# 608 slots an expert, logits by token, and half-width value products in the left units

## The chip, the cores and the metric

The kernel runs on one core of a Trainium2 chip. Its time is the device time of one execution in microseconds (us), and the median of several executions is what two kernels are compared by. A core has a matrix engine (PE, with its weight loads shown apart as PEld), a vector engine (DVE), an activation engine (ACT), a general engine (POOL, which also issues the indirect DMAs) and SP, which issues the plain DMAs. Each engine works through its own list of instructions in a fixed order; semaphores make one wait for another.

## The reference

Attention that keeps the 32 largest scores of a row, a feed-forward layer, and a mixture of experts in which each token goes to its two best experts of eight:

```python
# attention: q, k, v are (4, 8, 576, 64)
scores = scale * np.matmul(q, k.transpose(0, 1, 3, 2))
kth = np.partition(scores, -32, axis=-1)[..., -32:-31]
scores = np.where(scores >= kth, scores, -1e9)
attn = softmax(scores)
x = (attn @ v).transpose(0, 2, 1, 3).reshape(2304, 512)
# feed forward: w_in (512, 2048), w_out (2048, 512)
h = np.maximum(x @ w_in, 0.0)
x = h * h @ w_out
# mixture of experts: w1 (8, 512, 1024), w2 (8, 1024, 512)
noisy = x @ w_gate + np.log1p(np.exp(x @ w_noise)) * noise
top2 = the two largest of noisy, top2_w = softmax over them
for e in range(8):
    for k in range(2):
        mask = top2[:, k] == e
        h = np.maximum(x[mask] @ w1[e], 0.0)
        out[mask] += top2_w[mask, k, None] * (h @ w2[e])
```

## The kernel before, in words

**Attention** goes through 80 units. A full unit (`pair_full`, 64 of them) takes 128 queries of two heads. Since 576 is four and a half times 128, 64 queries of each batch and head are left over; a left unit (`pair_left`, 16 of them) takes these 64 queries of two heads at once, head A in rows 0 to 63 and head B in rows 64 to 127. `scores` (L363) makes the scores, DVE searches the 32 largest (L376 to L383), POOL and ACT make the softmax (L404, L405), `transpose4` (L417) and `rest` (L440, L441) turn the result, and `times_v` (L454) multiplies by the values: five chunks of keys times two heads, each a plain fp32 product that PE carries out as two instructions, with 64 value columns of one head as the loaded weights and 128 query columns moving through. In a left unit both heads move all 128 query columns, though `finish` (L430) reads only columns 0 to 63 of head A and 64 to 127 of head B.

**Feed forward** runs as filler between the attention steps (`ffn`, in six chunks of 384 tokens; L274 to L276 and L288 to L290) and is completed once attention has ended. Numbers that need more precision than one fp32r product gives are split into a high and a low part, so each product stands as three matmuls.

**The router** (`route`) follows each chunk. For each of its three tiles of 128 tokens it turns the tokens (L177, L179), multiplies with the 16 router columns as loaded weights and 128 tokens moving (L183), copies the 16 x 128 logits out (L184), and after the third tile turns all logits back by three small transposes (L188) and a copy (L191). The PSUM buffer `pf` that these steps and the feed-forward products use during attention is a single one. Then come small operations, and each token's row is written to two slots of `xs` by an indirect DMA (L251).

**The experts** have 640 static slots each, in five tiles of 128 that form two parts of 384 and 256 (`CAP`, `PARTS`). `fetch` reads a tile of slots, turns it (four transposes, L525) and splits it (L529, L530). `expert` runs eight steps over the 1024 hidden columns. In each step it loads and splits the weights (L567 to L572), makes 12 matmuls for the first part and 12 for the second (L578 to L580, the loaded weights being a 128 x 128 block of w1 and the tokens moving), splits the hidden values (L584, L585), and makes 15 matmuls with 512 moving columns, three for each tile (`second`, L559 to L561). At the end of an expert DVE adds each tile to the rows of the output gathered before (L599, three buffers `y`), and POOL scatters it (L600). Unused slots carry a row number beyond the end, which the indirect DMA skips. The first parts of experts 0 and 1 are worked on early, before the last chunk is routed; their second parts follow.

**Overflow**: if an expert gets more tokens than it has slots, a branch after the experts (`blank`, `beyond`) works on the rest in loops; otherwise it is jumped over.

The instructions are put in order by a list scheduler that plays the program through with modelled durations; an order number that the program gives (and the offsets `FILL_LATER` and `SOON`) decides among those that are ready.

Of the kernel before, what the change touches and what calls it, by code (L numbers as in the profile page):

```python
# [8 lines left out]
F32 = mybir.dt.float32  # L9
# [8 lines left out]
P = 128  # L18
# [34 lines left out]
def attention_ffn_moe(ctx: ExitStack, tc: tile.TileContext, q, k, v, w_ffn, w_route, noise, w_exp, out,  # L53
# [18 lines left out]
    CAP = 640  # L72
    CAPT = CAP // P
# [38 lines left out]
    nz = cpool.tile([P, NTT, E], F32, name="nz")  # L112

# [56 lines left out]
    def route(t0, xrs):  # L170

        nt = len(xrs)
        lts = fpool.tile([2 * E, CH], F32, name="lts", bufs=1)
        for i, xr in enumerate(xrs):
# [274 lines left out]
    def times_v(b, hA, pts, t5):  # L449
        av = ps_a.tile([P, 512], F32, name="pa")  # L450
        for c in range(NFULL + 1):
            for i in range(2):
                rhs = pts[i][:, c * P:(c + 1) * P] if c < NFULL else t5[:, 0, :]
                nc.tensor.matmul(av[i * D:(i + 1) * D, 0:P], V[b][c][:, hA + i, :], rhs,  # L454
                                 start=(c == 0), stop=(c == NFULL))
        return av, t5[:, 1, :]

    def pair_full(b, j, qt):
# [17 lines left out]
        yield times_v(b, hA, pts, t5)  # L476

    def pair_left(b, j, qt):
# [21 lines left out]
        yield times_v(b, hA, [pt, pt], t5)  # L500
# [14 lines left out]
    def fetch(e, parts):  # L515

        xe = [mpool.tile([P, 2, NC, n], F32R, name=f"xe{o}") for o, n in parts]
        t0, t1 = parts[0][0] // P, sum(parts[-1]) // P
        info = mpool.tile([P, CAPT, 4], F32, name="info")
        for t in range(t0, t1):  # L520
            xr = mpool.tile([P, ROW], F32, name="mr", bufs=3)
            nc.sync.dma_start(xr, xs[e * NT + t * P:e * NT + (t + 1) * P, :])
            pt = ps_m.tile([P, DM], F32, name="ph")
            for c in range(NC):
                nc.tensor.transpose(pt[:, c * P:(c + 1) * P], xr[:, c * P:(c + 1) * P], ident)  # L525
            i, off = place(parts, t)
            hi, lo = xe[i][:, 0, :, off:off + P], xe[i][:, 1, :, off:off + P]
            pv = pt.rearrange("p (c s) -> p c s", c=NC)
            nc.scalar.activation(hi, pv, AF.Copy)  # L529
            nc.vector.tensor_tensor(lo, pv, hi.bitcast(F32), op=ALU.subtract)  # L530
            gate(info[:, t, :], xr, e)
# [5 lines left out]
    def expert(e, parts, ahead):  # L537

        xe, info = found.pop(0)
        tiles_ = range(parts[0][0] // P, sum(parts[-1]) // P)  # L540
# [14 lines left out]
        def second(f, wo, hs):  # L555
            for t in tiles_:
                i, off = place(parts, t)
                sl = slice(off, off + P)
                nc.tensor.matmul(acc[t], hs[i][:, 0, sl], wo[:, 0, :], start=(f == 0), stop=False)  # L559
# [428 lines left out]
```

## Time and profile before

| what | us |
| --- | --- |
| median of three executions | 1397.62 |
| lowest and highest of them | 1397.25 to 1398.67 |
| the profiled execution | 1400.53 |
| its span, first to last instruction | 1398.8 |
| PE busy | 1272.1 (91%) |
| PEld busy | 1092.8 (78%) |
| DVE busy | 933.5 (67%) |
| ACT busy | 846.2 (60%) |
| POOL busy | 763.2 (55%) |

The profile is of one execution. Busy time of PE is modelled from pipelined matmuls: the duration of one matmul runs from its start to its last result, and the next has started long before, so what a matmul costs is read from the distance between two starts, not from its duration. The span falls into stages: attention with feed forward and conversion of weights up to about 800 us, the rest of feed forward and the early experts up to about 980 us, and the experts to the end.

### The profile page before, as it was taken

The numbers are of one execution on the slowest core, as the hardware profiler recorded it, in microseconds if no ns is written. First come the engines' busy times: TensorE is split into PE (matmuls) and PEld (weight loads), VectorE is DVE, ScalarE is ACT, GpSimd is POOL, SyncE is SP. The second block draws the span as 40 slices with busy tenths as digits, with TensorE's granted clock in tenths as the row PEclk, the third lists the DMA queues.
The fourth block names the chain that finished last, engine by engine and source line by source line (L and its number), as shares of the span: only waits on it lengthen the run. The fifth ranks groups of instructions, "written<-read, shape, count | busy, mean of one in ns | idle before, by whom it ended". The sixth has DMA issues, their size and how long they took to land.

```text
span 1398.8 us, 26295 instructions
## 1 busy us (share of the span) xinstructions
PE 1272.1 (91%) x7937; PEld 1092.8 (78%) x7937; DVE 933.5 (67%) x5089; ACT 846.2 (60%) x1757; POOL 763.2 (55%) x1238
## 2 busy tenths in 40 slices
PE   2766577999999999999999999899999999999996
PEld 1544465888888888878888888788888999989995
DVE  7999889799977999999889101145554444444342
ACT  5787898778877787988878434353443333233321
POOL 5868999655786577768647523605233405134131
PEclk9995688999999999999999999999999999999998
DMA  9985676653576355446524676837664334343241
GB/s 333 364 323 199 219 271 227 198 176 106 170 245 234 101 168 186 152 136 206 174 77 160 233 254 209 267 106 234 200 210 146 128 112 165 125 148 129 91 145 38
DMA packets 85240, 257.49 MB, mean 184 GB/s; under 512 B 10716, under 2 KB 10844, under 8 KB 85088
## 3 DMA queue, kind: packets, MB, share of 16 engines
q1 hardware_dynamic: 75808, 227.32, 48.8%
q0 software_dynamic: 9280, 28.40, 5.6%
q8 instruction: 65, 1.06, 0.3%
q14 instruction: 87, 0.71, 0.2%
HBM read 205.71 MB, written 52.06 MB: 184 GB/s over the span
## 4 chain that ended last, share of the span: by engine, by line
PE 59%; DVE 12%; DMA 4%; ACT 3%; POOL 3%; issue 2%; another core or an unknown queue 0%; SPq 0%; POOLq 0%; DVEq 0%; ACTq 0%
PE ph L579 5%; PE ph L578 5%; PE ph L580 5%; PE acc L559 5%; PE acc L561 5%; PE acc L560 5%; PE acc L276 4%; DVE w L377 3%; PE acc L274 3%; PE acc L275 3%; PE pa L454 3%; PE ps L363 3%; DVE m L376 3%; PE pa L417 2%; PE pf L288 2%; PE pf L290 2%
## 5 line engine op out<-in xcount | busy, mean ns | idle before, releaser
L404 POOL TENSOR_TENSOR sb<-sb,w 128x576 f32<-128x576 f32 x144 | 204.4, 1426 | 37.6 <-ACT w L403 36.6
L377 DVE MATCH_REPLACE8 w<-m,sb 128x96 f32<-128x96 f32 x864 | 202.5, 244 | 0.7 <-issue 0.6
L584 ACT ACTIVATE ht<-ph 128x384 fp32r<-128x384 f32 (+1 forms) x128 | 55.9, 437 | 217.3 <-PE ph L580 202.7
L585 DVE SCALAR_TENSOR_TENSOR ht<-ph,ht 128x384 fp32r<-128x384 f32 (+1 forms) x128 | 62.7, 490 | 183.7 <-ACT ht L584 171.0
L376 DVE MAX8 m<-sb 128x8 f32<-128x96 f32 x864 | 168.6, 246 | 21.7 <-ACT sb L365 15.3
L363 PE MATMUL ps<-K,qt 128*128 128x288 f32 (+2 forms) x640 | 139.9, 349 | 41.6 <-ACT sb L365 15.8
L600 POOL DMA_INDIRECT out<-y,info x40 | 45.1, 1128 | 241.3 <-DVE y L599 234.7
L578 PE MATMUL ph<-xe,wi 128*128 128x384 f32 (+1 forms) x512 | 159.9, 312 | 2.0 <-DVE xe L530 2.0
L579 PE MATMUL ph<-xe,wi 128*128 128x384 f32 (+1 forms) x512 | 160.1, 313 | 0.8 <-DVE xe L530 0.8
L580 PE MATMUL ph<-xe,wi 128*128 128x384 f32 (+1 forms) x512 | 159.4, 311 | 0.0
L363 PEld LDWEIGHTS ps<-K,qt 128*128 128x128 f32 x640 | 107.8, 215 | 58.9 <-ACT sb L365 24.3
L298 POOL TENSOR_TENSOR gt<-r,gt 128x384 fp32r<-128x384 f32 x96 | 97.2, 1014 | 84.4 <-ACT gt L297 68.6
L559 PE MATMUL acc<-wo,ht 128*128 128x512 f32 x320 | 126.7, 398 | 1.2 <-DVE y L599 0.7
L405 ACT ACTIVATE sb<-sb,keep 128x576 f32<-128x576 f32 x144 | 111.7, 776 | 23.3 <-POOL sb L404 22.8
L560 PE MATMUL acc<-wo,ht 128*128 128x512 f32 x320 | 125.4, 394 | 0.0
L403 ACT ACTIVATE w<-sb,keep 128x576 f32<-128x576 f32 x144 | 110.2, 774 | 21.7 <-POOL keep L399 19.3
L417 PE MATMUL pa<-ident,sb 128*128 128x128 f32 x576 | 101.5, 304 | 23.0 <-ACT sb L405 17.0
L288 PE MATMUL pf<-xT,wi 128*128 128x384 f32 x320 | 114.2, 357 | 4.1 <-DMA wi<-wsc 2.3
L274 PE MATMUL acc<-wo,gt 128*128 128x512 f32 x288 | 112.1, 402 | 4.8 <-DMA wo<-wsc 2.9
L289 PE MATMUL pf<-xT,wi 128*128 128x384 f32 x320 | 110.8, 346 | 2.8 <-POOL xT L432 2.7
L290 PE MATMUL pf<-xT,wi 128*128 128x384 f32 x320 | 111.0, 347 | 0.0
L275 PE MATMUL acc<-wo,gt 128*128 128x512 f32 x288 | 110.1, 396 | 0.0
(185 smaller groups left out, 3437.4 us busy)
## 6 DMA issues: line engine op xcount, KB each, us to landing
wi<-wsc SPq DMA_DIRECT2D x96, 512.0 KB, 4.9
wo<-wsc SPq DMA_DIRECT2D x96, 512.0 KB, 4.1
raww<-in_exp SPq DMA_DIRECT2D x80, 512.0 KB, 3.6
raw<-in_ffn SPq DMA_DIRECT2D x32, 512.0 KB, 4.7
wsc<-csp SPq DMA_DIRECT2D x32, 512.0 KB, 5.4
xs<-xr SPq DMA_DIRECT2D x40, 258.0 KB, 6.8
mr<-xs SPq DMA_DIRECT2D x40, 258.0 KB, 3.7
qn<-in_q SPq DMA_DIRECT2D x40, 256.0 KB, 2.8
```

The source lines that it names most:

```text
L274: nc.tensor.matmul(acc[tt], gt[:, 0, sl], wo[:, 0, :], start=(f == 0), stop=False)
L275: nc.tensor.matmul(acc[tt], gt[:, 0, sl], wo[:, 1, :], start=False, stop=False)
L288: nc.tensor.matmul(ph[:, 0:n], wi[:, 0, sl], xT[:, 0, c, 0:n], start=(c == 0), stop=False)
L363: nc.tensor.matmul(ps[:, n, 0:w], st, kt[:, at:at + w], start=(i == 0), stop=(i == len(pairs) - 1))
L376: nc.vector.max(top, sb[:, sl])
L377: nc.vector.match_replace(out=w[:, sl], in_to_replace=top, in_values=sb[:, sl], imm_value=NEG)
L404: nc.gpsimd.tensor_tensor(sb, sb, w, op=ALU.subtract)
L559: nc.tensor.matmul(acc[t], hs[i][:, 0, sl], wo[:, 0, :], start=(f == 0), stop=False)
L560: nc.tensor.matmul(acc[t], hs[i][:, 0, sl], wo[:, 1, :], start=False, stop=False)
L578: nc.tensor.matmul(ph[:, 0:n], wi[:, 0, sl], xe[i][:, 0, c, :], start=(c == 0), stop=False)
L579: nc.tensor.matmul(ph[:, 0:n], wi[:, 0, sl], xe[i][:, 1, c, :], start=False, stop=False)
L580: nc.tensor.matmul(ph[:, 0:n], wi[:, 1, sl], xe[i][:, 0, c, :], start=False, stop=(c == NC - 1))
```

## The change

Three things are changed.

1. `CAP` goes from 640 to 608. The parts are now 384 and 224, the fifth tile has 96 rows. Its transposes, matmuls, splits and the final addition are cut to 96 rows; the unused 32 rows of its `info` get a row number beyond the end, and the last 32 rows of its `y` are set to zero by a POOL memset before the addition.
2. The router's product has the turned tokens as loaded weights (128 x 128) and the 16 router columns moving, so the logits come out with a token in each row. The copy goes straight into `lgs`; the three transposes back (L188) and the copy after them (L191) are gone.
3. In a left unit, `times_v` moves only the 64 query columns of each head.

The overflow branch is adapted to a first slot that is not a multiple of 128.

```diff
-    CAP = 640
-    CAPT = CAP // P
+    CAP = 608
+    CAPT = -(-CAP // P)
     PARTS = [(0, 384), (384, CAP - 384)]
...
     def route(t0, xrs):
-        lts = fpool.tile([2 * E, CH], F32, name="lts", bufs=1)
+        lgs = fpool.tile([P, CT, 2 * E], F32, name="lgs", bufs=2)
...
-                nc.tensor.matmul(lt[0:2 * E, 0:P], wg[:, c, :], xt[:, c, :], start=(c == 0), stop=(c == NC - 1))
-            nc.scalar.copy(lts[:, i * P:(i + 1) * P], lt[0:2 * E, 0:P])
+                nc.tensor.matmul(lt[:, 0:2 * E], xt[:, c, :], wg[:, c, :], start=(c == 0), stop=(c == NC - 1))
+            nc.scalar.copy(lgs[:, i, :], lt[:, 0:2 * E])
             yield 1
-        lp = ps_f.tile([P, DM], F32, name="pf")
-        for i in range(nt):
-            nc.tensor.transpose(lp[:, 2 * E * i:2 * E * (i + 1)], lts[:, i * P:(i + 1) * P], ident[0:2 * E, 0:2 * E])
-        lgs = fpool.tile([P, CT, 2 * E], F32, name="lgs", bufs=1)
         lg = lgs[:, 0:nt, :]
-        nc.scalar.copy(lg, lp[:, 0:2 * E * nt].rearrange("p (t e) -> p t e", e=2 * E))
...
-    def times_v(b, hA, pts, t5):
+    def times_v(b, hA, pts, t5, whole):
         av = ps_a.tile([P, 512], F32, name="pa")
         for c in range(NFULL + 1):
             for i in range(2):
-                rhs = pts[i][:, c * P:(c + 1) * P] if c < NFULL else t5[:, 0, :]
-                nc.tensor.matmul(av[i * D:(i + 1) * D, 0:P], V[b][c][:, hA + i, :], rhs,
+                o, n = (0, P) if whole else (i * LEFT, LEFT)
+                rhs = pts[i][:, c * P + o:c * P + o + n] if c < NFULL else t5[:, 0, o:o + n]
+                nc.tensor.matmul(av[i * D:(i + 1) * D, o:o + n], V[b][c][:, hA + i, :], rhs,
                                  start=(c == 0), stop=(c == NFULL))
...
     def fetch(e, parts):
+            n = min(P, CAP - t * P)
-            nc.sync.dma_start(xr, xs[e * NT + t * P:e * NT + (t + 1) * P, :])
+            nc.sync.dma_start(xr[0:n], xs[e * NT + t * P:e * NT + t * P + n, :])
...
-                nc.tensor.transpose(pt[:, c * P:(c + 1) * P], xr[:, c * P:(c + 1) * P], ident)
+                nc.tensor.transpose(pt[:, c * P:c * P + n], xr[0:n, c * P:(c + 1) * P], ident[0:n, 0:n])
...
+            if n < P:
+                nc.gpsimd.tensor_copy(info[n:P, t, 3:4].bitcast(I32), far[n:P])
...
         def second(f, wo, hs):
-                sl = slice(off, off + P)
+                sl = slice(off, off + rows[t])
+                to = acc[t][0:rows[t]]
...
             y = mpool.tile([P, DM], F32, name="y", bufs=3)
-            nc.vector.scalar_tensor_tensor(y, acc[t], info[:, t, 2:3], cur[t], op0=ALU.mult, op1=ALU.add)
+            n = rows[t]
+            if n < P:
+                nc.gpsimd.memset(y[n:P], 0.0)
+            nc.vector.scalar_tensor_tensor(y[0:n], acc[t][0:n], info[0:n, t, 2:3], cur[t][0:n],
+                                           op0=ALU.mult, op1=ALU.add)
```

## Rows read from the trace of the kernel before

**Rows 1.** By stretch: length, busy us (count) of PE, PEld, DVE, ACT, POOL, clock, DMA

```profile
300.00:480.00 180.00, 176.25 (x1275) 148.96 (x1275) 152.63 (x1031) 143.12 (x312) 123.91 (x191) 1.00 0.52 175
480.00:640.00 160.00, 154.46 (x1123) 132.56 (x1120) 155.67 (x1101) 135.03 (x293) 112.92 (x185) 0.99 0.46 154
640.00:800.00 160.00, 159.39 (x1140) 137.15 (x1138) 123.46 (x845) 121.91 (x268) 102.98 (x165) 1.00 0.49 165
1100.00:1384.00 284.00, 284.00 (x1613) 256.81 (x1612) 118.82 (x199) 88.64 (x176) 81.58 (x168) 1.00 0.38 123
```

**Rows 2.** Chain that ended last, shares by line, 480 to 640 and 640 to 800 us

```profile
by line: DVE w L377 23.4%; DVE m L376 17.6%; DVE m L378 11.5%; DVE cand L383 10.1%; DVE m L381 9.2%; issue 3.8%; ACT sb L365 2.1%; ACT pt L419 1.8%; POOL sb L404 1.8%; ACT sb L405 1.6%; DVE x L426 1.5%; ACT w L403 1.5%; ACT r L296 0.9%; DVE
by line: PE pa L454 14.2%; PE pa L417 10.3%; PE ps L363 10.3%; PE acc L274 9.8%; PE pf L288 9.8%; PE pf L290 9.6%; PE acc L276 9.6%; PE pf L289 9.6%; PE acc L275 9.6%; PE pf L183 1.8%; PE pa L440 1.3%; PE pa L441 1.3%; PE pf L177 1.0%; DVE 
```

**Rows 3.** Instruction groups by form: operation, shapes, count, busy us, mean ns

```profile
L578 PE MATMUL ph<-xe,wi 128*128 128x256 f32 x256 | 73.2, 286 | 2.0 <-DVE xe L530 2.0
L363 PE MATMUL ps<-K,qt 128*128 128x64 f32 x64 | 13.0, 203 | 0.0
```

**Rows 4.** Timeline of PE within an expert: start us, duration us, instruction

```profile
1157.73 0.28 PE L578 MATMUL ph<-xe,wi 128*128 128x256 f32 x1
...
1159.15 0.40 PE L559 MATMUL acc<-wo,ht 128*128 128x512 f32 x1
...
1161.00 0.34 PE L578 MATMUL ph<-xe,wi 128*128 128x384 f32 x1
...
1163.12 0.86 PE L561 MATMUL acc<-wo,ht 128*128 128x512 f32 x3
```

**Rows 5.** Chain of 707 to 736 us, a left unit: start us, us, what

```profile
712.23 1.29 PE ps L363 x8
...
713.77 1.02 PE pa L454 x16
...
715.91 0.37 PE pa L454 x4
...
716.87 0.98 PE pf L183 x8
```

**Rows 6.** Timeline of PE, the router's count products

```profile
948.47 0.17 PE L222 MATMUL pf<-mb,onesb 128*128 128x8 bf16 x1
948.50 0.17 PE L223 MATMUL pf<-mb,tri 128*128 128x8 bf16 x1
```

**Rows 7.** Timeline of PE around one set of transposes back

```profile
937.93 0.34 PE L578 MATMUL ph<-xe,wi 128*128 128x384 f32 x1
938.20 0.35 PE L188 MATMUL pf<-ident,lts 16*128 16x16 f32 x3
...
938.77 0.34 PE L580 MATMUL ph<-xe,wi 128*128 128x384 f32 x1
```

**Rows 8.** Copies of a left unit's scores: count, min/median/max ns, first and last start

```profile
L367 ACT ACTIVATE sb<-ps x16: 570/597/625, 136.6 to 725.2; 128x512 f32<-128x512 f32 x16
```

**Rows 9.** Timeline of the end: DVE's additions and POOL's scatters

```profile
1390.99 1.46 DVE L599 SCALAR_TENSOR_TENSOR y<-acc,info,cur 128x512 f32<-128x512 f32 x2 [3.64 <-DMA out<-y,info]
1392.02 0.98 POOL L600 DMA_INDIRECT out<-y,info  x1 [0.95 <-DVE y L599]
1393.30 0.98 POOL L600 DMA_INDIRECT out<-y,info  x1 [0.30 <-issue]
```

**Rows 10.** Timeline between two experts: additions of the fourth and fifth tile, next product

```profile
1160.03 0.74 DVE L599 SCALAR_TENSOR_TENSOR y<-acc,info,cur 128x512 f32<-128x512 f32 x1
...
1163.82 0.40 PE L559 MATMUL acc<-wo,ht 128*128 128x512 f32 x1
```

**Rows 11.** Indirect DMA by window: packets, MB; expert 1's second part, expert 7 whole

```profile
q0 software_dynamic: 160, 0.43, 15.2%
...
q0 software_dynamic: 400, 1.21, 22.9%
```

**Rows 12.** Instruction groups: POOL clearing a whole 128x512 tile

```profile
L545 POOL MEMSET cur<- 128x512 f32 x6 | 2.9, 528 | 0.1
```

More of the change, by code (lines that the diff above doesn't have):

```diff
@@ L112, in attention_ffn_moe @@
     nz = cpool.tile([P, NTT, E], F32, name="nz")
+    far = cpool.tile([P, 1], F32, name="far")
+    nc.gpsimd.memset(far, float(2 * NT))
     wctx = ctx.enter_context(ExitStack())
@@ L475, in pair_full @@
         yield
-        yield times_v(b, hA, pts, t5)
+        yield times_v(b, hA, pts, t5, True)
     def pair_left(b, j, qt):
@@ L499, in pair_left @@
         yield
-        yield times_v(b, hA, [pt, pt], t5)
+        yield times_v(b, hA, [pt, pt], t5, False)
     def place(parts, t):
@@ L517, in fetch @@
         xe = [mpool.tile([P, 2, NC, n], F32R, name=f"xe{o}") for o, n in parts]
-        t0, t1 = parts[0][0] // P, sum(parts[-1]) // P
+        t0, t1 = parts[0][0] // P, -(-sum(parts[-1]) // P)
         info = mpool.tile([P, CAPT, 4], F32, name="info")
@@ L521, in fetch @@
             xr = mpool.tile([P, ROW], F32, name="mr", bufs=3)
-            nc.sync.dma_start(xr, xs[e * NT + t * P:e * NT + (t + 1) * P, :])
+            n = min(P, CAP - t * P)
+            nc.sync.dma_start(xr[0:n], xs[e * NT + t * P:e * NT + t * P + n, :])
             pt = ps_m.tile([P, DM], F32, name="ph")
             for c in range(NC):
-                nc.tensor.transpose(pt[:, c * P:(c + 1) * P], xr[:, c * P:(c + 1) * P], ident)
+                nc.tensor.transpose(pt[:, c * P:c * P + n], xr[0:n, c * P:(c + 1) * P], ident[0:n, 0:n])
             i, off = place(parts, t)
-            hi, lo = xe[i][:, 0, :, off:off + P], xe[i][:, 1, :, off:off + P]
-            pv = pt.rearrange("p (c s) -> p c s", c=NC)
+            hi, lo = xe[i][:, 0, :, off:off + n], xe[i][:, 1, :, off:off + n]
+            pv = pt.rearrange("p (c s) -> p c s", c=NC)[:, :, 0:n]
             nc.scalar.activation(hi, pv, AF.Copy)
             nc.vector.tensor_tensor(lo, pv, hi.bitcast(F32), op=ALU.subtract)
-            gate(info[:, t, :], xr, e)
+            gate(info[0:n, t, :], xr[0:n], e)
+            if n < P:
+                nc.gpsimd.tensor_copy(info[n:P, t, 3:4].bitcast(I32), far[n:P])
             yield None
@@ L539, in expert @@
         xe, info = found.pop(0)
-        tiles_ = range(parts[0][0] // P, sum(parts[-1]) // P)
+        tiles_ = range(parts[0][0] // P, -(-sum(parts[-1]) // P))
+        rows = {t: min(P, CAP - t * P) for t in tiles_}
         cur = {}
@@ L557, in second @@
                 i, off = place(parts, t)
-                sl = slice(off, off + P)
-                nc.tensor.matmul(acc[t], hs[i][:, 0, sl], wo[:, 0, :], start=(f == 0), stop=False)
-                nc.tensor.matmul(acc[t], hs[i][:, 0, sl], wo[:, 1, :], start=False, stop=False)
-                nc.tensor.matmul(acc[t], hs[i][:, 1, sl], wo[:, 0, :], start=False, stop=(f == NFE - 1))
+                sl = slice(off, off + rows[t])
+                to = acc[t][0:rows[t]]
+                nc.tensor.matmul(to, hs[i][:, 0, sl], wo[:, 0, :], start=(f == 0), stop=False)
+                nc.tensor.matmul(to, hs[i][:, 0, sl], wo[:, 1, :], start=False, stop=False)
+                nc.tensor.matmul(to, hs[i][:, 1, sl], wo[:, 0, :], start=False, stop=(f == NFE - 1))
                 yield True, 0.5
@@ L818, in attention_ffn_moe @@
     nc.vector.tensor_copy(first, row_i)
-    far = cpool.tile([P, 1], F32, name="far")
-    nc.gpsimd.memset(far, float(2 * NT))
     any_extra = nc.values_load(extra[0:1, E:E + 1], min_val=0, max_val=NT + P)
@@ L836, in blank @@
         nc.vector.tensor_tensor(taken, row, base[:, e:e + 1], op=ALU.is_lt)
+        outside = opool.tile([P, 1], F32, name="outside")
+        nc.vector.tensor_scalar(outside, row, float((e + 1) * NT), None, op0=ALU.is_ge)
+        nc.vector.tensor_tensor(taken, taken, outside, op=ALU.add)
         nc.vector.tensor_scalar(taken, taken, float(E * NT), None, op0=ALU.mult)
@@ L896, in attention_ffn_moe @@
                 nc.vector.tensor_scalar(row, first, float(e * NT), None, op0=ALU.add)
-                with tc.For_i(0, (NT - CAP) // P, 1):
+                with tc.For_i(0, -(-(NT - CAP) // P), 1):
                     blank(e, row, none)
```

## The prediction

> **What bounds the kernel now.** I read the busy time by stretch first, then the chain of what ended last in the same stretches, then the starts of single matmuls. From 1100 to 1384 us, six experts and part of a seventh, PE is busy without a gap at the full granted clock while DVE, ACT and POOL are busy less than half of the time [rows 1]. What PE saves there comes off the time one for one. From 640 to 800 us PE is busy 159.4 of 160 us, DVE 123.5, and the head of the chain is PE work alone [rows 1, 2]. From 480 to 640 us it is the other way round: DVE is busy 155.7 of 160 us and the chain is the search for the largest scores [rows 1, 2]; PE time saved in that stretch buys nothing. From 300 to 480 us PE is busy 176.3 of 180 us, with DVE at 152.6 behind it [rows 1]: mostly PE, with little room before DVE is next. The change touches PE's instructions in both kinds of stretch, and almost nothing of DVE's.
>
> **How a matmul is priced.** I take the distance between starts. Twelve matmuls of 256 columns take 1157.73 to 1159.15, 0.118 us each; eight of 512 take until 1161.00, 0.231 each; twelve of 384 take until 1163.12, 0.177 each [rows 4]. So a column costs some 0.45 ns with a small constant, and 224 columns would cost 0.118 - 32 x 0.00045 = 0.104 us. But each matmul also needs its own 128 x 128 block of weights loaded, and that has a floor. The scores of a left unit show it: four matmuls of 512 columns alternate with four of 64 [rows 3], and the eight take 1.29 us [rows 5]. Four of 512 are 0.93; the other four take 0.36, although 64 columns cost only about 0.03. The first 64-column matmul finds its weights loaded during the 512 before it (0.03); the other three wait about 0.11 each, the load behind a matmul too short to cover it. **A 128-column load cannot be repeated faster than about 0.111 us**, and 224 columns fall below this.
>
> **608 slots, first products.** The three lines have 256 matmuls of 256 columns each [rows 3], 768 in all, of which each goes from 0.118 to the floor of 0.111: 768 x 0.007 = 5.4 us. Ends: 768 x 0.014 = 10.8 us if the columns decide, nothing if the load already sets 0.118. I take the load's floor, since its row has the same kind of weights and is the nearest. The 64-column form also shows that fewer than 256 columns don't fall into a slower mode: four passes over 64 columns would not fit into 0.03 us.
>
> The Trainium skill ("TensorE: Matmul & The Clock Gate", Back-to-back issue gap, and LDWEIGHTS) gives a warm gap of N/2.4 + 2.5 ns and a load of columns/1.2 ns, so by it 256 columns cost 109 ns and the load 107: narrowing would gain 2 ns each, 1.5 us in all. The trace disagrees on the first figure, with 118 ns at 256 columns; this is the rival named B below.
>
> **608 slots, the rest.** The 15 products of the second kind still move 512 columns; 96 instead of 128 loaded columns lie under 0.231 us of moving: nothing. Four transposes of the fifth tile in each of eight experts move a quarter less: plain fp32 work takes 0.108 us for 128 columns (eight in 0.98, less the change of kind [rows 5]), so at most 32 x 0.027 = 0.9 us, and I take 0.6 (loads may hold it; end 0). ACT's and DVE's narrower splits lie beside a saturated PE, with DVE busy 42% there [rows 1]: nothing. POOL gets a copy and a memset for each expert. A memset of a whole tile takes 0.53 us [rows 12]; the one here covers 32 partitions but as many columns. It must wait until the second tile's scatter has read the same `y` buffer (three buffers, fifth tile), and behind it on POOL stand the fifth tile's scatter and the next expert's gathers. DVE's fifth addition now waits for it, and the next expert's matmul into that PSUM tile waits for the addition. Between experts this has room: the fifth addition starts at 1160.03 and lasts 0.74, the matmul starts at 1163.82 [rows 10], so 3 us lie free, and a memset queued behind the fourth scatter needs about 1. At the very end nothing covers it: the fourth scatter runs 1392.02 to 1393.00, and the fifth starts at 1393.30 since its addition was long done [rows 9]. With the memset (0.53) and the addition (0.75) in between it starts at about 1394.6, 1.3 us later; if the scheduler puts the memset ahead of the fourth scatter it costs nothing. I take 0.7 us, added. Slots suffice: expert 1's second part moves 0.43 MB in 2048-byte rows, about 208 beyond its 384, 592 in all; expert 7 moves 1.21 MB, 591 [rows 11], and the same windows of the other six show no more. All are below 608, so the overflow branch stays jumped over.
>
> **Left units.** From sixteen instructions in 1.02 us and four in 0.37 [rows 5], a pair of instructions (head A and head B, in different column halves) costs (1.02 - 0.37)/6 = 0.108 us, and the change of kind before them 0.15. Half the columns would halve the moving to 0.054; the load of 64 columns, half of 0.111, is about 0.055 (estimate), and the two loads of a pair go to different halves. Instructions can follow at this rate: two matmuls with loads of their own start 0.03 apart [rows 6], a pair 0.06. So 0.058 a pair, and the ten pairs of a unit save 0.5 us. The 16 left units run from 136.6 to 725.2 us [rows 8] in four groups of four, by batch: about 136 to 204, 309 to 354, 409 to 473 and 676 to 726 us. The first group runs before PE is the bound, the other three in the PE stretches. 12 x 0.5 = 6.0, and because DVE is close behind in the 300 to 480 stretch I count 5.0 us. Ends: nothing (DVE or loads hold it), 16 x 0.52 = 8.3.
>
> **Router.** One set of transposes back in expert surroundings: 937.93 to 938.77 for two products of 0.177 and the three transposes, so they cost 0.84 - 0.35 = 0.49 us with the changes of kind around them [rows 7]; where other plain fp32 work stands beside them, about 0.3. Six chunks give some 2.4, of which I count 1.8, as one or two lie in the DVE stretch; ends 0 and 2.9. The copy after them and a step on the single `pf` buffer go as well, beside other work. The turned product itself: eight instructions take 0.98 [rows 5], 0.108 each plus the change of kind. Now a 128-column load stands where 128 columns moved, 0.111 each: 18 x 8 x 0.003 = 0.4 us more, taken as 0.3; ends 0 and, if the loads don't overlap with the short matmuls at all, another 0.03 each, 4 us.
>
> **Sum.** 5.4 + 0.6 + 5.0 + 1.8 - 0.7 - 0.3 = 11.8 us off. Against the profiled execution: 1400.5 to 1388.7. That execution was 0.2% above the median, so against the median 1397.6 - 11.8 = **1386 us**.
>
> **Rivals.**
> A. *DVE takes over in attention.* The left units and the router save PE time, but DVE is 85% busy at 300 to 480 and 97% after [rows 1], so only the third group of left units and the last two chunks count: 2.0 + 0.8 instead of 6.8, 4.0 less, 1390. For it: the DVE stretch follows directly. Against: the chain at 640 to 800 is PE's. Chance 0.23.
> B. *The load already sets 0.118 at 256 columns,* so the narrower products bring nothing: 1391. Against it: 256, 384 and 512 columns lie on one line [rows 4], which a load floor would break, and the alternating scores give 0.111. Chance 0.10; the skill's figures above lead here.
> C. *Columns decide,* the load is no floor: 5.4 more, 1380. Only the scores' rows speak against it. Chance 0.10.
> D. *Another order of the work.* The scheduler plays the whole program through, so changed durations of the router and left units from 130 us on may change the order of everything behind them, attention's balance of PE and DVE included. PE's gaps from 300 to 640 us are 9 us [rows 1]; an order that doubles them takes most of the gain: 1395. Chance 0.07; an order that closes them goes the other way, about 1378, chance 0.05.
> E. *Slower: POOL's memset holds PE.* If the wait for the scatter's landing and POOL's queue delay the fifth addition beyond the 3 us of room [rows 10], PE stands at each of the seven expert boundaries. To lose more than 11.8 + 2.8 us it takes 2 us at each, a delay of 5 us: only if POOL has the memset behind the next expert's gathers. Then 1401. Chance 0.04.
> F. *Slower: fewer than 256 columns run in a slow mode,* at the rate of the plain fp32 rows (0.108 for 128 columns in each of two instructions [rows 5]): 224 columns would take 0.38 us, 768 x 0.26 = 200 us more, 1590. The 64-column form speaks against it. Chance 0.02.
>
> **How the numbers follow.** The forecast has 0.39; its own range is 1382 to 1389.5. What a measurement of this kernel can tell from no change is 0.2%, 2.8 us: 1394.8 to 1400.4. Forecast, A, B, C, the better half of D and half of its worse half are faster: 0.39 + 0.23 + 0.10 + 0.10 + 0.05 + 0.02 = 0.89; I keep a little for delays that no row shows: 0.85 faster, 0.08 the same, 0.07 slower. The range reaches over C below and most of D above: 1378 to 1395.
>
> **What would show it.** Right: starts of 224-column matmuls 0.111 apart, pairs of 64-column value products 0.058 apart, L188 gone, an expert 0.7 us shorter, attention ending 5 to 7 us earlier, the last scatter about a microsecond later after PE's end. Wrong: starts 0.104 or 0.118 apart; attention ending where it did with more idle PE; PE idle before a product into the fifth tile at the expert boundaries; new gaps in feed forward at 800 to 980 us; any work in the overflow branch.

## The result, and the profile after

The changed kernel takes 1410.7 us (1408.3 to 1416.5), the kernel before 1397.6 beside it: a ratio of 1.0080 (95% interval 1.0056 to 1.0104). It is slower by some 11 to 13 us, where 11.8 us less were forecast. The profiled execution took 1408.5 us, of which the span is 1406.8, against 1400.5 and 1398.8 before.

What the prediction said of single instructions came out as written. In the timeline of PE inside an expert (start us, duration us, instruction), twelve matmuls of 224 columns take from 1203.83 to 1205.16, 0.111 us each, where [rows 4] had 0.118:

```profile
1203.19 0.34 PE L583 MATMUL ph<-xe,wi 128*128 128x384 f32 x1
...
1203.83 0.27 PE L581 MATMUL ph<-xe,wi 128*128 128x224 f32 x1
...
1205.16 0.41 PE L562 MATMUL acc<-wo,ht 128*128 128x512 f32 x1
```

In the chain of what ended last (start us, us, what) from 460 to 469 us, a left unit's scores take 1.29 us as before, its values 0.61 and 0.27 instead of 1.02 and 0.37 [rows 5], and the router's product 0.80 instead of 0.98:

```profile
460.83 1.29 PE ps L360 x8
462.12 0.61 PE pa L452 x16
...
464.35 0.27 PE pa L452 x4
...
467.22 0.80 PE pf L185 x8
```

A pair of value products costs (0.61 - 0.27)/6 = 0.057 us (forecast 0.058), a unit saves 0.51 us (0.5), and a full expert, measured between the last additions of neighbouring experts, takes 57.4 to 58.1 us (four of them) where it took 57.9 to 58.8. These pieces of work became shorter by what was forecast, and the router's part by more. The loss lies elsewhere. The table by stretch (length; busy us of PE, PEld, DVE, ACT, POOL; granted clock; DMA) shows that PE stands idle more:

```profile
300.00:480.00 180.00, 172.71 (x1237) 146.98 (x1235) 147.98 (x1005) 137.03 (x301) 119.58 (x183) 0.98 0.50 171
480.00:640.00 160.00, 152.58 (x1104) 133.19 (x1102) 153.59 (x1068) 133.14 (x289) 113.36 (x188) 0.98 0.47 158
640.00:800.00 160.00, 157.36 (x1141) 135.91 (x1140) 133.28 (x898) 122.16 (x268) 103.41 (x166) 1.00 0.48 166
800.00:980.00 180.00, 169.81 (x923) 151.82 (x923) 41.52 (x117) 76.14 (x153) 71.17 (x155) 0.99 0.63 211
980.00:1100.00 120.00, 109.86 (x636) 95.25 (x636) 59.61 (x106) 47.48 (x96) 35.23 (x93) 0.94 0.52 172
1100.00:1384.00 284.00, 284.00 (x1631) 253.01 (x1631) 120.38 (x203) 89.87 (x179) 86.38 (x179) 1.00 0.39 126
```

The kernel before, in the two stretches that [rows 1] doesn't have:

```profile
800.00:980.00 180.00, 173.41 (x916) 150.53 (x914) 45.95 (x124) 76.84 (x151) 67.90 (x148) 0.99 0.65 216
980.00:1100.00 120.00, 113.74 (x668) 101.72 (x667) 60.64 (x105) 47.27 (x95) 35.48 (x91) 0.97 0.53 174
```

Length less PE's busy time is PE idle: from 300 to 1100 us it is 37.7 us after and 22.8 before, 14.9 more, spread over every stretch but the last. That sum alone doesn't tell what was lost: with the same work in the order of before it is 35.0 us in a faster kernel (below), so much of it is saved work that became idle time. The granted clock, a mean of its two levels of 1.2 and 2.4 GHz as a share of the upper one, fell as well: 0.98, 0.98 and 0.94 instead of 1.00, 0.99 and 0.97 in the first, second and fifth stretch. Lengths times the missing clock are 15.8 us after and 7.0 before, so up to 8.8 us of full-speed work more were lost in that way; PE had idled more in those stretches. The end costs 1.3 us more: from the start of the last two additions to the end of the span 9.1 us, before 7.8 [rows 9]. The clearing of `y` stands there as feared, between the last two scatters:

```profile
1398.75 0.97 POOL L607 DMA_INDIRECT out<-y,info  x1 [0.83 <-DVE y L605]
1399.71 0.55 POOL L604 MEMSET y<- 32x512 f32 x1
1400.54 0.97 POOL L607 DMA_INDIRECT out<-y,info  x1 [0.28 <-POOL y L604]
```

By milestones of the two profiled executions, in us after less us before: last scores +18.7 (782.9 against 764.2), last second-layer product of the feed forward +7.6, last scatter into `xs` +5.9, first addition of expert 0's second part +9.7, of expert 1's second part +11.1, last pair of additions of the last expert +6.7, the span +8.0. So attention ends much later with part of the feed forward done earlier, the experts' first boundaries lose 5 us more, and the full experts win 4 back.

### The profile page after: what moved, and what is told of

It is laid out like the page before. It is cut to its first block, busy times and chain, and to the rows that moved or that the text cites. A ratio compares the mean times of both kernels' runs of the same rounds, so it can differ in the third digit from the quotient of the medians.

```text
span 1406.8 us, 26264 instructions
## 1 busy us (share of the span) xinstructions
PE 1263.8 (90%) x7919; PEld 1086.3 (77%) x7919; DVE 934.5 (66%) x5089; ACT 840.0 (60%) x1751; POOL 767.5 (55%) x1254
## 4 chain that ended last, share of the span: by engine, by line
PE 60%; DVE 13%; DMA 13%; POOL 5%; ACT 4%; issue 3%; SPq 1%; another core or an unknown queue 0%; POOLq 0%; DVEq 0%; ACTq 0%
PE acc L562 5%; PE acc L564 5%; PE acc L563 5%; PE ph L583 5%; PE ph L582 5%; PE ph L581 5%; DVE w L374 4%; PE pa L452 4%; PE acc L271 4%; PE acc L272 3%; PE acc L273 3%; DMA xs<-xr 3%; PE ps L360 3%; PE pf L285 3%; DVE m L373 3%
## 5 line engine op out<-in xcount | busy, mean ns | idle before, releaser
L374 DVE MATCH_REPLACE8 w<-m,sb 128x96 f32<-128x96 f32 x864 | 205.5, 255 | 0.1
L373 DVE MAX8 m<-sb 128x8 f32<-128x96 f32 x864 | 171.7, 257 | 28.8 <-ACT sb L362 25.9
L562 PE MATMUL acc<-wo,ht 128*128 128x512 f32 (+1 forms) x320 | 127.5, 402 | 1.2 <-ACT ht L587 1.2
L563 PE MATMUL acc<-wo,ht 128*128 128x512 f32 (+1 forms) x320 | 126.1, 397 | 0.0
L271 PE MATMUL acc<-wo,gt 128*128 128x512 f32 x288 | 114.4, 411 | 7.2 <-DMA wo<-wsc 6.0
L285 PE MATMUL pf<-xT,wi 128*128 128x384 f32 x320 | 113.3, 354 | 2.4 <-DMA wi<-wsc 1.3
L414 PEld LDWEIGHTS pa<-ident,sb 128*128 128x128 f32 x576 | 71.5, 154 | 53.4 <-ACT sb L402 24.0
L286 PE MATMUL pf<-xT,wi 128*128 128x384 f32 x320 | 109.7, 343 | 2.6 <-POOL xT L429 2.6
L272 PE MATMUL acc<-wo,gt 128*128 128x512 f32 x288 | 111.3, 400 | 0.0
```

The source lines that it names most:

```text
L271: nc.tensor.matmul(acc[tt], gt[:, 0, sl], wo[:, 0, :], start=(f == 0), stop=False)
L285: nc.tensor.matmul(ph[:, 0:n], wi[:, 0, sl], xT[:, 0, c, 0:n], start=(c == 0), stop=False)
L373: nc.vector.max(top, sb[:, sl])
L374: nc.vector.match_replace(out=w[:, sl], in_to_replace=top, in_values=sb[:, sl], imm_value=NEG)
L414: nc.tensor.transpose(pt[:, c * P:(c + 1) * P], e[:, c * P:(c + 1) * P], ident)
L562: nc.tensor.matmul(to, hs[i][:, 0, sl], wo[:, 0, :], start=(f == 0), stop=False)
```

## The experiments

A comparison of medians has an uncertainty of some 0.2%; each ratio stands against the kernel before on the same chip. Line numbers differ by a few between kernels.

### One part at a time

The change was split into its three parts, each applied alone.

> The kernel before with the slots alone at 608 (router and left units as before). Theory 'order': the matrix work of an expert gets 0.7 us shorter as in the changed kernel, attention keeps its order, so 1397.6 - 5 = 1392 to 1393. Theory 'experts': the added POOL memset or the smaller fifth tile costs at the boundaries, so 1400 or more.

> The kernel before with the router alone changed. Theory 'order': the scheduler gives another order of attention, feed forward and early experts, and the time moves by 5 us or more either way, with PE's idle time in 300 to 640 us different from the 9 us of before. Theory 'work': only the instructions count, 1.5 to 2 us less: 1396.

> The kernel before with the left units alone changed. Theory 'order': attention ends at another time than the work removed explains (more than 5 us off), later than before although PE has 6 us less to do. Theory 'work': 1397.6 - 5 = 1392.5.

| alone, in the scheduler's order | ratio | 95% interval |
|---|---|---|
| 608 slots | 1.0004 | 0.9983 to 1.0026 |
| router | 1.0064 | 1.0041 to 1.0086 |
| left units | 0.9992 | 0.9969 to 1.0015 |

The part with the least work in it, the router, carries most of the loss, and neither of the other two brings its 5 us. Yet its product got cheaper and its transposes are gone. What also differs between these kernels and the one before is the order: the scheduler lists the instructions of every engine anew from their modelled durations, and in the traces of the router's and the left units' kernels some 2300 and 2000 of PE's 7900 places hold work on another tile than before. With the slots alone it is some 50. So the slots keep PE's order and still gain nothing, as their second theory had it (1400 or more). The router's moved by more than 5 us, as its first theory had it, but its idle PE from 300 to 640 us is 9.6 us, as before, and not another. The left units' met neither theory: no 5 us less, and attention ends at 763.3 us, 0.9 earlier.

### The same work in the order of before

For the next kernels the scheduler's order for the kernel before was written down, and each instruction of the changed program was tied to its predecessor in that list. Such a tie fixes the order of issue on an engine and adds no wait. Instructions that are gone leave no trace in it; new ones are put behind the one that they follow in the program.

```diff
     wctx.close()
+    if keep is not None:
+        in_order(nc, tc)
```

> The left units' values with 64 columns a head, and nothing else; every engine's instructions (PE, DVE, ACT, POOL, SP) are issued in exactly the order of the kernel before, instead of the order that the scheduler works out for the changed sizes. Theory 1, the scheduler's other order eats what the narrower matmuls save: 4 to 6 us less than the kernel before (the pairs of 64-column value products start 0.058 us apart instead of 0.108). Rival 2, the saved PE time was never on the path (each left unit then waits for what feeds it): within 1 us of the kernel before, as the same work in its own order was (0.9992).

> The router with the tokens stationary, and nothing else, in the order of the kernel before on every engine (the three transposes and the copy of each chunk that are gone leave their places empty). Theory 1, the order: the 9 us that this part cost in its own order are gone, and the time is 1 to 5 us less than the kernel before (18 transposes back are gone, 8 products take 0.80 instead of 0.98 us). Rival 2, the router's new work itself is dearer, or its logits come late: 6 to 10 us more than the kernel before, as in its own order (1.0064).

> The changed kernel, all of it, with POOL's copy and clearing as they are, but with the order of the kernel before on every engine. Theory 1, the other order is most of the loss and POOL's copy some 4 us: within 3 us of the kernel before, so 8 to 14 us less than the changed kernel. Rival 2, the order matters for the router alone and not for the sum: 5 us or more above the kernel before.

| in the order of before | ratio | 95% interval | own order |
|---|---|---|---|
| left units | 0.9981 | 0.9961 to 1.0001 | 0.9992 |
| router | 0.9956 | 0.9938 to 0.9974 | 1.0064 |
| the whole change | 0.9972 | 0.9957 to 0.9986 | 1.0080 |

The router's new form is 6 us faster in one order and 9 slower in the other, with the same instructions. The whole change, untouched but for the order, is faster than the kernel before: order is worth 1.1%, about 15 us. For the left units alone the two intervals overlap; there nothing is shown, and 3 us less is below the 4 to 6 of theory 1. The router gained a little more than its theory had (6 us, against 1 to 5), and the whole change too (4 us less than before, where within 3 was expected).

In the waits of PE (us in total, times, longest) of the router alone, from 300 to 960 us, first in its own order and then in that of before, one sees what a worse order can look like. In the first, PE stands before the feed forward for the activations `r` and the weights `wi`, `wo`, 19.4 us in the three longest sums; in the second these come to 4.3 us, and its longest sums are short waits for ACT and POOL. The trace of the first is of its quickest execution (1402.0 us of a median of 1408.3), so it shows the smaller part of the loss.

```profile
PE pf L283 <- ACT r L289: 9.7, 7, 3.9
PE acc L269 <- DMA wo<-wsc: 5.3, 3, 2.2
PE ph L283 <- DMA wi<-wsc: 4.4, 2, 4.1
```

```profile
PE ps L358 <- ACT sb L360: 2.9, 2, 1.8
PE acc L271 <- POOL gt L293: 2.5, 3, 1.3
PE pa L449 <- ACT pt L414: 2.1, 4, 1.1
PE pf L283 <- DMA wi<-wsc: 1.6, 1, 1.6
PE ph L283 <- DMA wi<-wsc: 1.5, 2, 1.0
PE pa L412 <- DVE x L421: 1.2, 2, 0.8
PE pf L283 <- ACT r L289: 1.2, 1, 1.2
```

Which engine's list is it? The same kernel with PE's alone put back:

> The router alone, with the order of the kernel before on PE only; ACT, DVE, POOL and SP are left to the scheduler. It tells which engine's order cost the 9 us. Theory 1, PE's (second-layer products of the feed-forward ahead of the scores that the search waits for): as with the order of before on every engine (0.9956). Rival 2, that of POOL, DVE or the queues: 4 to 9 us more than the kernel before.

It measures 0.9991 (0.9969 to 1.0014): PE's order gives back some two thirds of the way from 1.0064 to 0.9956. That the rest hangs on the other engines' lists is likely, but the intervals of 0.9991 and 0.9956 overlap. Theory 1 had expected all of it.

### Order with no work changed

Two kernels have exactly the instructions of the kernel before; one constant each moves where feed-forward work is strewn into attention.

```diff
-RATE = 6.0
+RATE = 5.9
```

```diff
-LEFT_WEIGHT = 0.6
+LEFT_WEIGHT = 0.58
```

> The kernel before, the same instructions on the same operands, in a slightly other order: the constant by which feed-forward work is spread over the attention units is 5.9 instead of 6.0. As many positions in PE's order differ as with the router's new form. Theory 1, order alone moves this kernel's time by several us: anything from 4 us less to 12 us more than the kernel before, and not within 2 us in both of the two runs of this kind. Rival 2, order is neutral and what the changed kernels lost was something else in them: within 2 us in both runs.

> The kernel before, the same instructions on the same operands, in another slightly other order: the weight of a left unit in the spreading of the feed-forward work is 0.58 instead of 0.6. Theory 1: 4 us less to 12 us more than the kernel before, and not within 2 us in both of the two runs of this kind. Rival 2: within 2 us in both.

They take 1.0022 (1.0007 to 1.0038) and 1.0061 (1.0038 to 1.0084) of the time before. Nothing is computed otherwise, and 3 and 8 us are gone, the first of them little above the uncertainty. The second is as bad as the router's new form in its own order. In its profile the last scores start at 774.0 us, 9.8 later than before, and every full expert takes 57.8 to 59.1 us, as before: as in the changed kernel, what is lost is lost before them. Rival 2 of these runs falls.

What the lost time consists of differs. PE's idle time is the span less its busy time. In the two trials it is 5.7 and 8.6 us more than before, in spans 4.5 and 7.9 longer, and in the router's kernel 7.7 us more than with the same work in the old order, in a span 9.4 longer: there the loss is idle PE, or most of it. For the whole change it is not. Busy times of the changed kernel, span 1406.8, and of the same work in the order of before, span 1395.8:

```profile
PE 1263.8 (90%) x7919; PEld 1086.3 (77%) x7919; DVE 934.5 (66%) x5089; ACT 840.0 (60%) x1751; POOL 767.5 (55%) x1254
PE 1250.9 (90%) x7919; PEld 1076.4 (77%) x7919; DVE 929.8 (67%) x5089; ACT 839.7 (60%) x1751; POOL 765.1 (55%) x1254
```

Idle PE is 143.0 and 144.9 us (35.0 from 300 to 1100 us in the second, 37.7 in the first): the 11 us between these two executions are busy time, for the same instructions. Up to the last scatter into `xs` the changed kernel is 13.2 us behind (966.4 against 953.2), more than the whole. Its mean granted clock over all executions is 0.947 against 0.950, and its PE stream goes 518 instead of 495 times from one kind of product to another; by estimate that is some 4 us of full-speed work (0.003 of 1400) and some 2 us (0.1 us a change, as the router's sets show below), so about half stays open.

### POOL's copy at the first boundaries

The 608 slots need a small copy: it writes the number of the far slot into `info`, rows 96 to 127 of the fifth tile. Here it is moved to DVE.

```diff
-                nc.gpsimd.tensor_copy(info[n:P, t, 3:4].bitcast(I32), far[n:P])
+                nc.vector.tensor_copy(info[n:P, t, 3:4].bitcast(I32), far[n:P])
```

> 608 slots an expert alone, as in the run of that part before, but the small copy of the far slot's number into the rows 96 to 127 of the fifth tile is on DVE instead of POOL. Theory 1, the copy made POOL wait for the indirect gathers of the expert before, and that held the weight loads of the first experts: 3 to 5 us less than the kernel before. Rival 2, the 224-column products save nothing that reaches the end: within 1 us of the kernel before, as with the copy on POOL (1.0004).

It measures 0.9963 (0.9945 to 0.9981), 5 us less than before, against 1.0004 with the copy on POOL: theory 1 holds, and this is the 5.3 us that the prediction had for the slots. The timeline of POOL before expert 2 shows how a copy of 0.18 us can cost 4. With the copy on POOL:

```profile
1023.48 1.01 POOL L553 DMA_INDIRECT cur<-out,info  x1 [0.31 <-issue]
1024.59 1.02 POOL L509 TENSOR_SCALAR info<-mr 128x1 f32<-128x1 f32 x1
...
1028.61 0.18 POOL L536 CAST info<-far 32x1 int32<-32x1 f32 x1 [1.54 <-DMA cur<-out,info]
1028.88 1.94 POOL L512 TENSOR_SCALAR info<-info 128x1 f32<-128x1 f32 x3
...
1033.87 0.30 POOL L509 TENSOR_SCALAR info<-mr 128x1 f32<-128x1 f32 x1 [2.18 <-DMA mr<-xs]
```

With the copy on DVE:

```profile
1019.84 1.01 POOL L553 DMA_INDIRECT cur<-out,info  x1 [0.31 <-issue]
...
1022.89 0.47 POOL L512 TENSOR_SCALAR info<-info 128x1 f32<-128x1 f32 x3
...
1026.41 0.30 POOL L509 TENSOR_SCALAR info<-mr 128x1 f32<-128x1 f32 x1 [2.17 <-DMA mr<-xs]
```

The copy stands in the middle of the gates, ahead of L512, and waits for the gather issued just before to land. Of the 3.8 us by which this stretch is longer, the wait is 1.5, and L512 takes 1.94 us for its three instead of 0.47; why that is isn't shown. On DVE the copy waits for the scatters before the gathers instead, 21.2 us for all eight, and nothing on POOL stands behind it:

```profile
1017.73 0.15 DVE L536 CAST info<-far 32x1 int32<-32x1 f32 x1 [2.91 <-DMA out<-y,info]
```

Why the program sets the one wait there and the other here wasn't settled. The gates read the `mr` buffers; SP's next load into `mr` waits for them. From the last gather's start to the next tokens' gate it takes 10.4 us instead of 6.6. PE, which turns these tokens, stands for their load 5.35 us instead of 1.55 (first with the copy on POOL, then on DVE):

```profile
1033.90 0.87 PE L528 MATMUL ph<-ident,mr 128*128 128x128 f32 x3 [5.35 <-DMA mr<-xs]
```

```profile
1026.44 0.63 PE L528 MATMUL ph<-ident,mr 128*128 128x128 f32 x4 [1.55 <-DMA mr<-xs]
```

In [rows 10] no such chain can be seen, since later experts have their tokens fetched long before. Expert 0's and expert 1's second parts, the short ones, expose it:

| us between last additions | before | slots, POOL | slots, DVE | changed kernel |
|---|---|---|---|---|
| expert 0, second part | 32.3 | 35.7 | 32.0 | 35.5 |
| expert 1, second part | 28.8 | 32.2 | 28.1 | 30.2 |
| expert 3, whole | 58.4 | 57.9 | 57.5 | 58.1 |

### All three parts without the two losses

All parts, the copy on DVE, the order of before; the clearing of `y` follows the scatter that it follows in the program.

> All three parts of the change, the small copy on DVE, and the order of the kernel before on every engine. Theory 1 (the order and POOL's wait are the whole loss): 9 to 13 us less than the kernel before, the time that the sum of the saved work gave. Rival 2 (the saved work was not on the path, or the router's new form costs): within 3 us of the kernel before, or slower.

It gives 0.9968 (0.9948 to 0.9988), less than theory 1 wants and no better than the whole change in that order with the copy on POOL (0.9972): the medians don't show the copy's cost here, though the two profiles do, with 35.8 us for expert 0's second part with the copy on POOL and 32.7 with it on DVE. But expert 1's second part took 32.2 us again, and POOL's timeline at the end of expert 0's second part says why (first this kernel, then one in which the clearing may take any place):

```profile
1005.23 1.31 POOL L607 DMA_INDIRECT out<-y,info  x1 [18.88 <-DVE y L605]
1006.59 0.52 POOL L604 MEMSET y<- 32x512 f32 x1
1007.39 1.77 POOL L607 DMA_INDIRECT out<-y,info  x1 [0.28 <-POOL y L604]
1013.92 1.40 POOL L549 DMA_INDIRECT cur<-out,info  x1 [4.76 <-DMA out<-y,info]
```

```profile
1009.74 1.32 POOL L607 DMA_INDIRECT out<-y,info  x1 [18.15 <-DVE y L605]
1011.37 1.10 POOL L607 DMA_INDIRECT out<-y,info  x1 [0.31 <-DVE ht L588]
1016.84 1.12 POOL L549 DMA_INDIRECT cur<-out,info  x1 [4.36 <-DMA out<-y,info]
```

Between two scatters the clearing pushes the second one back, the gather waits for it to land, and the gates and loads wait behind the gather: 8.7 us from first scatter to gather, against 7.1. PE then stands for the load of the tokens 5.57 us, against 2.91:

```profile
1023.21 1.09 PE L524 MATMUL ph<-ident,mr 128*128 128x128 f32 x4 [5.57 <-DMA mr<-xs]
```

```profile
1025.76 0.63 PE L524 MATMUL ph<-ident,mr 128*128 128x128 f32 x4 [2.91 <-DMA mr<-xs]
```

> All three parts, the small copy on DVE, the order of the kernel before, but the clearing of rows 96 to 127 of y takes its place by itself: ahead of both scatters of expert 1's second part instead of between them. Theory 1, between the scatters it delayed the second one and with it the gather, the gates and the load of the next tokens (that part took 32.2 us against 28.1 where it stood ahead): 3 to 4 us less than the run with it between, 7 to 9 us less than the kernel before. Rival 2, the boundary is the transfers' own: 3 to 5 us less than the kernel before, as there.

This is 0.9932 (0.9909 to 0.9955), 1392.8 against 1400.8 us: theory 1. Expert 1's second part takes 28.7 us instead of 32.2, expert 0's 33.7 instead of 32.7. All three parts together bring 9.5 us by the ratio, the most of the three kernels with all parts in the old order. Its interval just touches that of the run before (0.9948 to 0.9988), and the profiled spans of the two are alike (1391.2 and 1390.8 us), so in the whole time the clearing's cost is less sure than at the boundary.

### Gathers and scatters of 96 rows

A way to need neither the copy nor the clearing is to move only the 96 rows that exist.

```diff
-                out=cu, out_offset=None, in_=out,
-                in_offset=bass.IndirectOffsetOnAxis(ap=info[:, t, 3:4].bitcast(I32), axis=0),
+                out=cu[0:rows[t]], out_offset=None, in_=out,
+                in_offset=bass.IndirectOffsetOnAxis(ap=info[0:rows[t], t, 3:4].bitcast(I32), axis=0),
...
-                out=out, out_offset=bass.IndirectOffsetOnAxis(ap=info[:, t, 3:4].bitcast(I32), axis=0),
-                in_=y, in_offset=None, bounds_check=NT - 1, oob_is_err=False),
+                out=out, out_offset=bass.IndirectOffsetOnAxis(ap=info[0:n, t, 3:4].bitcast(I32), axis=0),
+                in_=y[0:n], in_offset=None, bounds_check=NT - 1, oob_is_err=False),
```

> All three parts in the order of the kernel before, and the fifth tile's gather and scatter move only its 96 rows, so that neither the copy of the far slot's number nor the clearing of rows 96 to 127 of y is needed. Theory 1, POOL's two small additions lie in the chain scatter, gather, gate, load at the first experts' boundaries: 2 to 5 us less than with the copy on DVE (0.9968), that is 7 to 10 us less than the kernel before. Rival 2, those boundaries are set by the transfers alone: as with the copy on DVE, 3 to 6 us less than the kernel before.

> The changed kernel in the order that the scheduler gives it, with 96-row gathers and scatters for the fifth tile and without POOL's copy and clearing. Theory 1: the 3 to 5 us of the boundaries come back, the order's loss stays: 5 to 9 us more than the kernel before. Rival 2, the loss is POOL's copy in all: level with the kernel before or less.

Both theories fell: 1.0010 (0.9994 to 1.0026) in the order of before, 1.0155 (1.0121 to 1.0189) in the scheduler's own, 5 and 10 us worse than the 128-row forms (0.9972, 1.0080). The experts are hardly to blame: in the order of before the last additions started 2.7 us later than with the copy on DVE. But the end takes long. Its last scatter starts at 1387.07 in a span of 1403.3 us:

```profile
1387.07 0.94 POOL L603 DMA_INDIRECT out<-y,info  x1 [0.30 <-issue]
```

That is 16.3 us from the start of the last scatter to the end, and 16.2 in the other kernel of this form; with 128 rows and the copy on DVE it is 5.9 (1384.92 in 1390.8) and before 5.5 [rows 9]. It is not data that comes late: the last DMA packet ends at 1391.0, 12.3 us before the end, where it is 1.5 us in the two with 128 rows. What the end waits for is open.

### Is DVE the bound in attention?

Two attempts to take DVE work off the search without touching PE: move the addition of EPS to a unit's sums to POOL, or leave it out.

```diff
-                nc.vector.tensor_scalar(sm[:, i:i + 1], sm[:, i:i + 1], 1.0, EPS, op0=ALU.mult, op1=ALU.add)
+                nc.gpsimd.tensor_scalar(sm[:, i:i + 1], sm[:, i:i + 1], 1.0, EPS, op0=ALU.mult, op1=ALU.add)
```

> As the run with 96-row gathers in the order of the kernel before, and the addition of the small constant to a unit's sums (144 instructions of 0.142 us on DVE) is on POOL. It tests whether DVE has become what attention waits for. Theory A, DVE is the bound from 300 to 640 us, and what PE saved there became idle time: the 64 instructions of that stretch, 9 us, are on the path, and the time falls by 4 to 9 us against the run without the move. Theory B, PE or the transfers bound it: within 2 us of that run, or more where the small sums now wait for POOL.

> The kernel before in its own order, but without the addition of EPS to the sums of a unit (144 DVE instructions of 0.142 us, 64 of them from 300 to 640 us; this part of the computation is left out). Theory A, DVE bounds the attention from 300 to 640 us already, so that PE time saved there can't come through whole: 4 to 9 us less than the kernel before. Theory B, PE bounds it: within 2 us.

> As the run with all three parts and the clearing in a place of its own, but without the addition of EPS to the sums (as in the run of the kernel before without it; this part of the computation is left out). Theory A, with the left units and the router cheaper on PE, DVE holds more of the attention than before: 6 to 12 us less than the same kernel with the additions, more than the kernel before loses by the same edit. Theory B, PE bounds it still: within 2 us of the kernel with the additions.

The move says nothing of DVE's bound: 1.0174, 22 us slower than the form without it, and DVE's reciprocal now waits for POOL. DVE's waits, 300 to 770 us:

```profile
DVE sm L409 <- POOL sm L408: 28.9, 13, 9.0
```

Left out, the addition brings 0.9985 (0.9969 to 1.0001) in the kernel before, and 0.9921 (0.9892 to 0.9949) beside 0.9932 in the kernel with all parts. Both are nearer to theory B's 2 us than to theory A's 4 to 9 and 6 to 12, so DVE is at most a weak bound, before and after; the intervals reach to 4 us less and, between the last two kernels, further. What the trace does show is PE idle in the best kernel, from 300 to 640 us:

```profile
300.00:480.00 180.00, 173.12 (x1275) 148.96 (x1275) 153.00 (x1039) 143.74 (x314) 124.38 (x193) 1.00 0.54 178
480.00:640.00 160.00, 152.08 (x1116) 132.09 (x1115) 154.47 (x1094) 134.26 (x291) 112.15 (x185) 0.99 0.46 154
```

PE stands for 14.8 us there, 5.5 more than before [rows 1]: that much of the saved work became idle time. This list fixes how much feed forward stands between the units; whether another could fill the gaps is open.

## Why the prediction was wrong

**Most terms of the work were right.** 224 columns fall to the weight load's floor: 0.111 us, as taken from the scores' rows. The router's turned product shows the same floor with 16 moving columns: its eight loads of 128 columns start 0.112 us apart in the trace, so the moving columns don't decide. So rival B (0.118 stays) and rival C (0.104) fall, and F too. The Trainium skill ("TensorE: Matmul & The Clock Gate", LDWEIGHTS) has a load of columns/1.2 ns, 107 for 128 columns; the trace agrees within 5 ns. A pair of value products costs 0.057 us, an expert lost 0.7 to 0.8 us. Slots without the copy's wait bring 0.37% or 5 us (5.3 forecast with the tail), the left units 0.19% or 3 (5.0; the interval of 0.9961 to 1.0001 holds both that and nothing), the router in the old order 0.44% or 6 (1.5). All parts in the old order bring 9.5 us (6.3 to 12.7) where the sum had 11.8.

**The router's term was mis-sized with the wrong sign in one half.** The turned product was priced 0.3 us dearer for the load's floor. Instead, in the old order, 12 of its 18 sets of eight take 0.81 us from the first start to the next product's, where 17 of 18 took 0.98; all 18 together are 2.2 us shorter. One set after, one before:

```profile
831.44 0.96 PE L183 MATMUL pf<-wg,xt 128*128 128x16 f32 x8
832.25 0.42 PE L283 MATMUL ph<-xT,wi 128*128 128x384 f32 x1
```

```profile
835.97 1.05 PE L183 MATMUL pf<-xt,wg 128*16 128x128 f32 x8
836.94 0.44 PE L288 MATMUL ph<-xT,wi 128*128 128x384 f32 x1
```

The step between two starts was priced rightly (0.112 us, before 0.109). What the prediction left as it was are the ends of a set: the second start now follows the first after 0.03 us instead of 0.12, and the next product follows the last start after 0.11 instead of 0.20. The transposes back, priced at 1.8 us, took 1.9 in the kernel before, up to the next product's start. What makes up the rest of the 6 us isn't shown.

**The step that failed first: the sum kept the order and had no term for it, and rival D, which did, had 0.12 in all and 1395 us at its worse end.** D named the mechanism, that changed durations shift the order of everything behind them, and then priced it by the 9 us of gaps that [rows 1] showed from 300 to 640 us. But the gaps of a well-ordered kernel don't bound those of another order. Order cost 15 us (1.0080 against 0.9972) with the same work. With no work changed it cost 3 and 8 us in two trials of two. The worse half of D had a chance of 0.07, and at worst a time below that of the kernel before; each of these four orders (the changed kernel's, the router's, the two trials) is slower than the kernel before. Nor need it be gaps: of the 11 us between its profile and that of the same work in the old order, none is idle PE (143.0 against 144.9 us), and how the longer busy time divides is open.

**The step that failed second: POOL's copy and clearing, at nothing between the experts.** The clearing was priced by its duration and by the room at a boundary between whole experts [rows 10], and the copy had no price at all. The prediction didn't ask what the copy waits for, transfers in flight. And the boundary chosen was the roomiest; those behind the two short second parts have scatter, gather, gates, load and weights in one chain, and each of the two cost up to 4 us there. Rival E had POOL hold PE, by another wait, and at all seven boundaries. In the time of the changed kernel this is the smaller loss: its two boundaries are 3.2 and 1.4 us longer than before.

**The end** was right in kind: 1.3 us where 0.7 was taken and 1.3 was the upper end.

**Rival A** (DVE takes over) isn't settled. 5.5 us of PE's savings became idle time in attention, as it says; but DVE work left out brings only 2 to 3 us by the medians, which speaks against DVE as the cause.

## What to carry to other kernels

Where a scheduler lists instructions by modelled durations, any edit is two changes: the work and the order. Tie the new program to the old order to measure the work alone, and expect the order's part to be as large as a gain of 1%; both trials with no work changed were slower here. Price a small instruction on an in-order queue by what it waits for and by the tightest place where it stands, not by its duration at a roomy one.

## What the runs showed of the hardware

- The end of the program came 16 us after the start of the last indirect scatter of 96 rows, in all three kernels of that form, and 5.4 to 7.7 us after one of 128 rows, in all the others. With 96 rows the last packet had ended 12 us before.
- Clearing 32 partitions of 512 columns takes POOL 0.52 to 0.56 us, as long as 128 partitions (0.53 [rows 12]).
- Loads of 128 columns follow each other at 0.111 to 0.112 us behind 224 moving columns and behind 16 alike.
- With narrow products the router is faster, not slower: eight 128-column loads with 16 moving columns in 0.81 us in two thirds of the sets, where 16-column loads with 128 moving columns took 0.98.
